# Attention with a gated MLP on one core: loads of the output weights in head order, x in halves, and a new matmul order in the last stage

## The chip, the cores and the metric

The kernel runs on one core of a Trainium2 chip. The metric is device time in microseconds (us) of one execution, the median of many. Most executions of a kernel agree within about 0.3%. PE is TensorE (matmuls), PEld its weight loads, DVE VectorE, ACT ScalarE, POOL GpSimd, and SPq the queue on which the Sync engine issues DMAs.

## The reference

```python
x  = A_x                                   # (1, 2048, 512) bf16
xn = layernorm(x)
q  = xn @ wq                               # 32 heads of 128
k, v = last 512 rows of the caches         # 8 kv heads, each used by 4 heads
o  = softmax(q k^T / sqrt(128)) v          # per head
s  = concat(o) @ wo                        # (4096, 512)
g  = silu(silu(xn @ w1) @ w2)              # MLP 512 -> 1792 -> 512
return x + s * g
```

## The kernel before

The tokens are worked in 4 blocks of 512. A *step* is one head of one block, 128 steps in all. In each step PE computes a query projection (L207), four score matmuls (L229), four probability-times-value matmuls of the head three steps back (the *PV product*, L271), and filler: the MLP in block 0, the output projection of the block before (L328) later. ScalarE takes the exponentials, VectorE normalises them, and one transposing DMA per step, the *flip* `pT<-p_all`, turns them for the PV product. A flip is issued on SPq, in order with every other load on that queue:

```python
def flip(s):
    pT[s] = work.tile([P, NKC, BLK], BF16, name="pT", tag="pT", bufs=3)
    nc.sync.dma_start_transpose(
        pT[s].rearrange("p kc (j q) -> p (kc j) q", q=P), p_all[s][:, :, :, :]
    )
```

The output weights wo (32 heads of 128 KB) come on the same queue, over tiles that the MLP has left. Seven heads share one tile, in an order that forces some 384 KB to be loaded as two DMAs of 256 and 128 KB:

```python
WO_HOME = {"big0": (0, 1, 2, 3, 4, 5, 12), "big1": (6, 7, 8, 9, 10, 11, 13), ...}   # cut

wo_plan = {                       # at the end of step: [(first head, heads), ...]
    HQ - 5: [(0, 4)],
    HQ - 4: [(4, 2), (12, 1)],
    HQ - 3: [(6, 4)],
    HQ - 2: [(10, 2), (13, 1)],
    HQ + 1: [(14, 4)],
    HQ + 3: [(18, 2), (26, 1)],
    HQ + 5: [(20, 4)],
    HQ + 7: [(24, 2), (27, 1)],
    HQ + 9: [(28, 2), (30, 2)],
}
```

The output projection of the last block is not done head by head. It is a 2 x 2 scheme with seven products, m1 to m7, in place of eight. Each is two PSUM groups of 16 matmuls with 256 columns, one per pair of heads. VectorE prepares operands (`row_sums`, `diag`, `skew`) from the head outputs and combines the results. It begins while the last three PV products are still waiting for their flips:

```python
for u in pv_units(NSTEP - 2): u()              # the PV product before the last
for p in range(6, 12): diag(p)                 # VectorE
m34[4, 1] = bank("sc", [P, HALF], "m4_ps")
for p in range(EARLY): mm(m34[4, 1], 4, p, 1)  # 14 matmuls
for t in range(2):
    for p in (HP - 2, HP - 1): mm(m34[3, t], 3, p, t)   # 4 matmuls
for u in pv_units(NSTEP - 1): u()              # the last PV product
... # m5, rest of m4, then skew(0..9), m2, m1, m7, m6; cut
```

The softmax here doesn't subtract the row's maximum and nothing guards it: scores larger than these inputs give would overflow.

## Time and profile before

| | before |
|---|---|
| median of the executions first given, then of those timed beside the change | 555.18, 554.98 us |
| span of the profile | 552.5 us |
| PE busy | 541.3 us, 98% |
| PE waiting for flips, sum in the list of waits | 2.0 us in 3 waits |
| granted clock | 1.0 |

From the page of before: the span, the busy time per engine, and the chain that ended last, as shares of the span.

```profile
span 552.5 us, 8484 instructions
PE 541.3 (98%) x2629; PEld 260.7 (47%) x2676; DVE 461.0 (83%) x1261; ACT 387.5 (70%) x1122; POOL 20.4 (4%) x41
PE 91%; DMA 5%; DVE 1%; ACT 1%; issue 1%
```

PE is nearly always busy, so what can be gained without removing matmuls is the little time in which it isn't. From the timeline of PE in before, two windows. The columns are start, length, engine, line, operation, and in brackets the idle time just before and what ended it.

```profile
230.96 0.38 PE L229 MATMUL sc_ps<-kT,qT 128*128 128x512 bf16 x1
232.26 0.60 PE L271 MATMUL o_ps<-pT,v 128*128 128x512 bf16 x2 [0.92 <-DMA pT<-p_all]
...
528.90 0.27 PE L464 MATMUL m_ps<-wq_sum,oT 128*128 128x256 bf16 x1
529.82 1.02 PE L271 MATMUL o_ps<-pT,v 128*128 128x512 bf16 x4 [0.65 <-DMA pT<-p_all]
```

The bracket understates such a wait, because a matmul's shown length (0.38 us) runs past the start of the next one: matmuls of 512 columns start every 0.216 us, those of 256 every 0.109. This document therefore counts a wait as the distance of two starts less that pitch: 232.26 - 230.96 - 0.216 = 1.08 us, and 529.82 - 528.90 - 0.109 = 0.81 us. (The tables take starts to the nanosecond, hence 1.09.)

From the timeline of VectorE in before: its last instructions.

```profile
547.14 0.69 DVE L492 SCALAR_TENSOR_TENSOR x_t<-c,x_t 128x512 bf16<-128x512 f32 x1
547.75 0.42 DVE L488 TENSOR_TENSOR m<-m_ps,gate 128x256 f32<-128x256 f32 x1
548.20 0.42 DVE L585 SCALAR_TENSOR_TENSOR x_t<-m,c 128x256 bf16<-128x256 f32 x1
548.78 0.42 DVE L488 TENSOR_TENSOR m<-m_ps,gate 128x256 f32<-128x256 f32 x1 [0.16 <-PE m_ps L464]
549.24 0.43 DVE L585 SCALAR_TENSOR_TENSOR x_t<-m,c 128x256 bf16<-128x256 f32 x1
```

It waits only 0.16 us for PE: it is nearly a second limit of the last stage.

### The profile page before, as it was taken

Reading aid. Unit: us, or ns where it says so; the run is one execution under the profiler, and the core shown is the slowest. Engines: PE = TensorE matmul, PEld = TensorE weight load, DVE = VectorE, ACT = ScalarE, POOL = GpSimd, SP = SyncE. Lnnn points to the kernel's source line nnn. Section 1 sums busy time; section 2 is a strip of 40 time slices with the busy share of each in tenths; the row PEclk is TensorE's granted clock in tenths of the full one; section 3 lists DMA queues with packets and bytes.
Section 4 is the critical chain, followed back from the end, with each engine's and each line's share of the span. In section 5 each row is a group of like instructions: output and inputs, shape, how many; then the busy total and the mean of one; then the engine's idle time right before and its main releaser. Section 6 shows DMA issues by size and latency. Waiting matters only on the chain.

```text
span 552.5 us, 8484 instructions
## 1 busy us (share of the span) xinstructions
PE 541.3 (98%) x2629; PEld 260.7 (47%) x2676; DVE 461.0 (83%) x1261; ACT 387.5 (70%) x1122; POOL 20.4 (4%) x41
## 2 busy tenths in 40 slices
PE   8999999999999999999999999999999999999997
PEld 5644444444444444444444444444444444444576
DVE  6888978967896788798889888988889889888887
ACT  5458657756776677777777777777788888788600
POOL 1000000000000000010001000100010001000000
PEclk9999999999999999999999999999999999999999
DMA  9748697886859799979798979897989887988931
GB/s 295 184 104 171 132 194 150 175 171 135 161 114 182 181 208 222 205 147 185 153 149 162 183 154 150 162 184 153 152 160 178 160 146 158 179 154 134 182 87 39
DMA packets 297901, 89.69 MB, mean 162 GB/s; under 512 B 282368, under 2 KB 296960, under 8 KB 297856
## 3 DMA queue, kind: packets, MB, share of 16 engines
q1 hardware_dynamic: 296128, 85.09, 80.5%
q0 software_dynamic: 1312, 3.67, 2.5%
q8 instruction: 21, 0.34, 0.3%
q10 hardware_dynamic: 416, 0.39, 0.2%
q14 instruction: 24, 0.20, 0.1%
HBM read 17.30 MB, written 2.10 MB: 35 GB/s over the span
## 4 chain that ended last, share of the span: by engine, by line
PE 91%; DMA 5%; DVE 1%; ACT 1%; issue 1%
PE sc_ps L229 19%; PE o_ps L271 19%; PE q_ps L207 19%; PE s_ps L328 14%; PE oB_ps L176 9%; PE h_ps L144 6%; DMA pT<-p_all 5%; PE m_ps L464 4%; PE h_ps L658 2%; ACT th L154 1%; DMA x<-in_A_x_dram 1%; ACT p_all L232 0%; DVE hT L155 0%; DVE st L108 0%; PE t_ps L622 0%
## 5 line engine op out<-in xcount | busy, mean ns | idle before, releaser
L232 ACT ACTIVATE p_all<-sc_ps 128x512 bf16<-128x512 f32 x512 | 304.9, 597 | 99.0 <-PE sc_ps L229 84.4
L229 PE MATMUL sc_ps<-kT,qT 128*128 128x512 bf16 x512 | 193.7, 379 | 0.7
L244 DVE TENSOR_SCALAR p_all<-p_all,rden 128x512 bf16<-128x512 bf16 x512 | 157.8, 351 | 9.1
L271 PE MATMUL o_ps<-pT,v 128*128 128x512 bf16 x498 | 134.3, 379 | 2.6 <-DMA pT<-p_all 2.0
L207 PE MATMUL q_ps<-xnT,wq 128*128 128x512 bf16 x501 | 135.0, 379 | 0.5
L277 DVE CAST oT<-o_ps 128x512 bf16<-128x512 f32 x128 | 88.2, 689 | 44.0 <-PE o_ps L271 41.5
L232 ACT ACTIVATION_READ_ACCUMULATOR p_all<-sc_ps 128x1 f32 x512 | 101.0, 197 | 0.0
L328 PE MATMUL s_ps<-wo_big,oT 128*128 128x512 bf16 x326 | 97.8, 379 | 0.5
L271 PEld LDWEIGHTS <-v 128*128 128x128 bf16 x512 | 49.5, 98 | 63.6 <-DMA pT<-p_all 5.1
L229 PEld LDWEIGHTS <-qT 128*128 128x128 bf16 x512 | 50.1, 98 | 61.6 <-issue 1.8
L219 DVE CAST qT<-q_ps 128x512 bf16<-128x512 f32 x112 | 77.0, 687 | 2.5 <-PE q_ps L207 2.5
L207 PEld LDWEIGHTS <-wq 128*128 128x128 bf16 x512 | 50.1, 98 | 61.0 <-issue 1.0
L176 PE MATMUL oB_ps<-w,hT 128*128 128x512 bf16 x215 | 62.6, 379 | 0.3
L328 PEld LDWEIGHTS <-oT 128*128 128x128 bf16 x384 | 37.6, 98 | 45.3
L144 PE MATMUL h_ps<-xnT,w 128*128 128x512 bf16 x165 | 51.5, 379 | 0.6 <-DVE hT L155 0.3
L242 DVE RECIPROCAL rden<-den 128x2 f32<-128x2 f32 x256 | 40.5, 158 | 10.3 <-ACT p_all L232 10.3
L155 DVE SCALAR_TENSOR_TENSOR hT<-th,h_ps 128x512 bf16<-128x512 bf16 x42 | 28.8, 685 | 7.2 <-ACT th L154 6.9
L176 PEld LDWEIGHTS <-hT 128*128 128x128 bf16 x224 | 21.9, 98 | 26.2
L154 ACT ACTIVATE th<-h_ps 128x512 bf16<-128x512 f32 x42 | 25.1, 599 | 6.6 <-PE h_ps L144 5.7
L144 PEld LDWEIGHTS <-w 128*128 128x128 bf16 x168 | 16.4, 98 | 20.0 <-issue 0.4
L185 ACT ACTIVATE th<-oB_ps 128x512 bf16<-128x512 f32 x16 | 9.5, 595 | 18.0 <-PE oB_ps L176 17.2
L345 POOL DMA_DIRECT2D out_dram<-x_e x12 | 6.6, 549 | 316.2 <-DVE rden L242 303.4
(63 smaller groups left out, 236.0 us busy)
## 6 DMA issues: line engine op xcount, KB each, us to landing
wq<-in_A_wq_dram SPq DMA_DIRECT2D x8, 512.0 KB, 3.9
w<-in_B_w_dram SPq DMA_DIRECT2D x3, 896.0 KB, 10.3
pT<-p_all SPq DMA_TRANSPOSE x128, 4.4
wo_big<-in_A_wo_dram SPq DMA_DIRECT2D x4, 512.0 KB, 4.2
x<-in_A_x_dram SPq DMA_DIRECT2D x3, 512.0 KB, 10.2
x_e<-in_A_x_dram POOLq DMA_DIRECT2D x12, 128.0 KB, 3.1
out_dram<-x_e POOLq DMA_DIRECT2D x12, 128.0 KB, 2.2
v<-in_A_v_cache_dram SPq DMA_DIRECT2D x8, 128.0 KB, 3.9
```

Of the source, the lines that this page charges most:

```text
L144: nc.tensor.matmul(h_ps[:, lo : lo + n], w1_sb[f // FH][:, c, (f % FH) * P : (f % FH + 1) * P], xnT[b][:, c, lo : lo + n], start=(c == 0), ...
L154: nc.scalar.activation(th, h_ps, ACT.Tanh, scale=0.5)
L176: nc.tensor.matmul(cur["ps"], hT[b][f // 2][:, f % 2, j * P : (j + 1) * P], w2_sb[f // FH][:, f % FH, :], start=(f == 0), stop=(f == NFC - 1),
L207: nc.tensor.matmul(cur["ps"], wq_sb[h // REP][:, c, (h % REP) * DH : (h % REP + 1) * DH], xnT[b][:, c, :], start=(c == 0), stop=(c == ND - 1),
L219: nc.vector.tensor_copy(qT[s], cur["ps"])
L229: nc.tensor.matmul(sc, qT[s][:, j * P : (j + 1) * P], kT[h // REP], start=True, stop=True)
L232: nc.scalar.activation(p_all[s][:, :, j, :], sc.rearrange("p (kc q) -> p kc q", q=P), ACT.Exp, scale=INV_SQRT_DH, accum_out=den[s][:, j : ...
L242: nc.vector.reciprocal(rden, den[s][:, j0 : j1 + 1])
L244: nc.vector.tensor_scalar_mul(p_all[s][:, :, j, :], p_all[s][:, :, j, :], rden[:, j - j0 : j - j0 + 1])
L271: nc.tensor.matmul(cur["ps"], v_sb[h // REP][:, kc, :], pT[s][:, kc, :], start=(kc == 0), stop=(kc == NKC - 1))
L277: nc.vector.tensor_copy(oT[s // 2][:, s % 2, :], cur["ps"])
L328: nc.tensor.matmul(acc[j], oT[(b * HQ + h) // 2][:, h % 2, j * P : (j + 1) * P], wo_of(h), start=(h == 0), stop=(h == HQ - 1),)
```

## The change

Its intent is to take PE's last waits away: put more matmuls between the last two PV products, and let the loads of wo disturb the flips less.

```diff
     def load_x(b):
         new_x(b)
-        nc.sync.dma_start(x_blk[b], x2[...].rearrange("(j p) d -> p j d", p=P))
+        xv = x2[ds(b * BLK, BLK), :].rearrange("(j p) d -> p j d", p=P)
+        for j in range(0, BLKT, BLKT if b == 1 else 2):
+            n = BLKT if b == 1 else 2
+            nc.sync.dma_start(x_blk[b][:, j : j + n, :], xv[:, j : j + n, :])
 ... WO_HOME
-        "big0": (0, 1, 2, 3, 4, 5, 12),       # and so on
+        "big0": tuple(range(0, 7)),           # 7..13, 14..20, 21..27
 ... B_PAIRS regrouped to suit (cut)
 ... wo_plan
-            HQ - 4: [(4, 2), (12, 1)],
-            HQ - 3: [(6, 4)],
-            HQ - 2: [(10, 2), (13, 1)],
+            HQ - 4: [(4, 3)],
+            HQ - 3: [(7, 4)],
+            HQ - 2: [(11, 3)],
             HQ + 1: [(14, 4)],
-            HQ + 3: [(18, 2), (26, 1)],
-            HQ + 5: [(20, 4)],
-            HQ + 7: [(24, 2), (27, 1)],
-            HQ + 9: [(28, 2), (30, 2)],
+            HQ + 3: [(18, 3)],
+            HQ + 5: [(21, 4)],
+            HQ + 7: [(25, 3)],
+            HQ + 9: [(28, 2)],
+            HQ + 10: [(30, 2)],
 ... tail, around the last PV product (cut)
+        for t in range(2):
+            group(5, t, "f")                  # m5: one PSUM bank per half
+        run(5, 0, EARLY[:14])
+        run(5, 1, EARLY[:4])                  # 18 matmuls of m5 before it
+        for p in range(4):
+            skew(p)                           # VectorE, before the last cast
         for u in pv_units(NSTEP - 1):
             u()
+        run(5, 1, EARLY[4:])                  # 10 matmuls ready at once
+        ...                                   # last pairs of m3, m4, m5 and 14 of m2 interleaved
-        tt(c12, m5, a, ALU.add)
-        tt(d, m5, b, ALU.add)
+        for t in range(2):
+            tt(c12[:, t, :], acc[5, t], a[:, t, :], ALU.add)
+            tt(d[:, t, :], acc[5, t], b[:, t, :], ALU.add)
```

In effect there are four edits: x blocks 2 and 3 in halves; wo in head order with four pairs of loads merged; the last two loads of wo on two steps (the *split*); and the tail.

## The prediction

> **What bounds the kernel now.** TensorE. The page gives PE 541.3 us busy of a 552.5 us span (98%) at full granted clock, and the chain that ended last is 91% PE. In the timeline 128x512 matmuls start every 0.216 us and the 256-column ones of the tail every 0.109 us, nearly without a gap. Outside the start (7.2 us) and the end (3.8 us after the last matmul) PE waits for little: the list of waits has 2.0 us of PE on the transposing DMA of the probabilities (pT<-p_all) in three places. The timeline puts them at 232.26 us (0.92 us), 482.25 (0.45) and 529.82 (0.65). So the ceiling is about 2 us, 0.4%.
>
> **What the change does.** No matmul is added or removed: the order listing has 5354 rows on PE before and after, 981 against 983 on VectorE, 82 against 79 on the SP queue.
>
> 1. Tail. Between the last two PV products stand 18 small matmuls; now 32. 14 x 0.109 = 1.5 us more cover, against 0.65 us of waiting: the wait at 529.82 should go, and the last matmul end about 0.8 us earlier (0.65 shown, the rest start-up of the waiting weight load). But VectorE is nearly the limit there: from 536.1 to 549.7 us it has a single gap, 0.16 us. Two 128x512 additions (0.60 us apart) become four of 128x256 (some 0.38 apart): +0.3 us. Skew and diagonal work (0.34 and 0.2 us each) moves ahead of the last cast, into 1.74 us of idle time. I estimate that VectorE's closing chain starts 0.8 us earlier and ends 0.3 to 0.6 us earlier.
>
> 2. Loads of wo. Bytes are the same; four 3-tile loads replace four pairs of loads, which saves issue time on a queue off the critical path. The last 512 KB, two 256 KB loads issued back to back at 223.6 and 224.7 us, are split over two head steps. The flip issued right behind them (225.28 us) took 6.94 us to land against a median of 4.4, and is the one PE waits for at 232.26. The Trainium skill (DMA: Bandwidth & Descriptors, "Issuing engines are not separate DMA queues") says that all transfers run on the same 16 DMA engines and interleave; this trace agrees: flips behind 384-512 KB loads land in 5.0 to 6.5 us. With half the bytes ahead, an estimated 4.8 to 5.5 us: the 0.92 us wait should shrink to at most 0.2. A 16 KB instruction fetch (229.65 us) fell into the same flip, so part may stay.
>
> 3. Loads of x blocks 2 and 3 in halves: landed at 18.0 and 20.7 us, first read at 27.1. Nothing.
>
> 4. Another grouping of pairs for the weight differences: same VectorE work, nothing.
>
> The wait at 482.25 stays (a flip of 7.41 us, with an instruction fetch at 480.4 in it and no wo load).
>
> **Sum.** 0.8 us (wait at 232) + 0.5 us (tail) = 1.3 us of 555.18: predicted 553.9 us, 8 in 10 between 552.9 and 555.2. Faster by over 2%: 0.01; within 2%: 0.98; slower by over 2%: 0.01.
>
> **Right or wrong in the profile.** PE waits for pT fall from 2.0 to some 0.5 us with the one at 482 left; no gap before the last PV; last matmul about 1.7 us earlier, last VectorE instruction 1.0 to 1.5 us earlier; VectorE gaps below 0.5 us in the last 12 us.
>
> **What would make it wrong.** The instruction fetch still delays the flip at 225 us; waits reappear at other flips, since the slack between a flip's landing and its PV product is set by PE's own pace; the longer VectorE queue delays the last cast; VectorE ends the tail no earlier.

## The result, and the profile after

| | before | after |
|---|---|---|
| median | 554.98 us (15 runs) | 551.74 us (10 runs) |
| ratio, 95% interval | | 0.9946 (0.9937 to 0.9955) |
| span of the profile | 552.5 us | 549.3 us |
| PE busy | 541.3 us | 540.8 us |
| granted clock | 1.0 | 1.0 |

Ratios are the mean time of one kernel's runs over that of the other's in the same rounds, so not quite the ratio of the medians. Executions over 1.5% slower than the fastest of the same kernel are left out of the means. The gain is 0.54%, about 3.0 us, where 1.3 were predicted; 551.74 lies below the stated range.

From the page of after: the same lines as of before.

```profile
span 549.3 us, 8482 instructions
PE 540.8 (98%) x2628; PEld 261.0 (48%) x2676; DVE 461.1 (84%) x1263; ACT 388.2 (71%) x1122; POOL 20.3 (4%) x41
PE 91%; DVE 4%; DMA 3%; issue 1%; ACT 1%
```

The same work, and a chain whose DMA share fell from 5% to 3% while VectorE's rose from 1% to 4%: VectorE now holds the end. From the timeline of PE in after, the windows that answer to the two waits (PV products at 230.75 and 528.51 us):

```profile
230.54 0.38 PE L230 MATMUL sc_ps<-kT,qT 128*128 128x512 bf16 x1
230.75 1.03 PE L272 MATMUL o_ps<-pT,v 128*128 128x512 bf16 x4
...
526.48 2.13 PE L465 MATMUL m_ps<-wo_big,s 128*128 128x256 bf16 x18
528.51 1.04 PE L272 MATMUL o_ps<-pT,v 128*128 128x512 bf16 x3
529.38 1.25 PE L465 MATMUL m_ps<-wo_big,s 128*128 128x256 bf16 x10
```

The wait at 232 is gone: 230.75 follows 230.54 at the usual pitch. So is that before the last PV product: 18 matmuls from 526.48 take 18 x 0.109 = 1.96 us, so 0.07 is left. From the timeline of VectorE in after, its last instructions:

```profile
545.12 0.42 DVE L489 TENSOR_TENSOR m<-m_ps,gate 128x256 f32<-128x256 f32 x1
545.57 0.42 DVE L594 SCALAR_TENSOR_TENSOR x_t<-m,c 128x256 bf16<-128x256 f32 x1
545.96 0.42 DVE L489 TENSOR_TENSOR m<-m_ps,gate 128x256 f32<-128x256 f32 x1
546.42 0.43 DVE L594 SCALAR_TENSOR_TENSOR x_t<-m,c 128x256 bf16<-128x256 f32 x1
```

VectorE has no gap left, and ends at 546.85, 2.82 us earlier than before. The span ends 2.46 us after that, where it was 2.83. So one part of the gain, 0.37 us, lies *behind* the last instruction that computes anything; the prediction had nothing there.

### The profile page after: what moved, and what is told of

Same layout as the page of the kernel before. It is cut to its first block, busy times and chain, and to the rows that moved or that the text cites. A ratio compares the mean times of both kernels' runs of the same rounds, so it can differ in the third digit from the quotient of the medians.

```text
span 549.3 us, 8482 instructions
## 1 busy us (share of the span) xinstructions
PE 540.8 (98%) x2628; PEld 261.0 (48%) x2676; DVE 461.1 (84%) x1263; ACT 388.2 (71%) x1122; POOL 20.3 (4%) x41
## 4 chain that ended last, share of the span: by engine, by line
PE 91%; DVE 4%; DMA 3%; issue 1%; ACT 1%
PE o_ps L272 20%; PE sc_ps L230 20%; PE q_ps L208 19%; PE s_ps L329 14%; PE oB_ps L177 9%; PE h_ps L145 6%; PE h_ps L667 2%; DMA pT<-p_all 2%; PE m_ps L465 2%; DVE c L489 1%; DVE s L442 1%; ACT th L155 1%; ACT p_all L233 0%; DVE hT L156 0%; DMA x<-in_A_x_dram 0%
```

## The experiments

Two theories stood. A: the change is worth what its removed waits are worth, and the rest of what the two profiles differ by is chance of single profiles. B: the whole difference is made by the change. Each run below gave one profile, and all but one were timed in five rounds. All gave correct results. The table collects, for all of them, the three quantities that turned out to matter. A wait is start to start less the pitch; below 0.06 us it counts as 0. "End gap" is from the end of VectorE's last instruction to the end of the span, both taken from the trace to the nanosecond. Each profile is of one execution, and the executions of one kernel differ by 1 to 3 us, so a single row is weak; what repeats over rows counts.

| kernel | what it is | ratio (95% interval) | wait near 232 us | wait before last PV | end gap |
|---|---|---|---|---|---|
| before | | | 1.09 | 0.81 | 2.83 |
| ctrl_before | before, again | 1.0015 (1.0002 to 1.0027) | 1.36 | 1.40 | 2.82 |
| tail_only | tail alone | 0.9989 (0.9976 to 1.0001) | 1.04 | 0 | 2.84 |
| loads_only | all but the tail | 0.9978 (0.9966 to 0.9990) | 0 | 0.91 | 2.47 |
| split_only | split alone | 0.9986 (0.9970 to 1.0001) | 0.90, at 236 | 1.31 | 2.83 |
| split_again | the same | one run | 0.90, at 236 | 1.61 | 2.84 |
| wo_only | wo edits alone | 0.9976 (0.9959 to 0.9992) | 0 | 1.26 | 2.59 |
| after | the change | 0.9946 (0.9937 to 0.9955) | 0 | 0.07 | 2.46 |
| after_again | the same | 0.9950 (0.9936 to 0.9964) | 0 | 0 | 2.46 |
| after_nosplit | change, split undone | 0.9957 (0.9941 to 0.9973) | 0 | 0 | 2.48 |
| unmerged | and merging undone | 0.9968 (0.9953 to 0.9982) | 1.10 | 0 | 2.73 |
| before_x6 | before, x in 8 pieces | 0.9990 (0.9976 to 1.0004) | 0.79, at 204 | 1.34 | 2.47 |
| tail_cover | part of the tail alone | 0.9997 (0.9979 to 1.0015) | 1.86 | 0 | 2.84 |
| after_spread | change, more loads spread | 0.9948 (0.9932 to 0.9963) | 0 | 0 | 2.46 |

### The control, and the change again

Edit: none (ctrl_before, after_again).

> The kernel before, submitted unchanged, as a control. Both theories: ratio 1.000 within 0.001. Theory A (the extra gain that the prediction missed is chance of single profiles: first x tile landing at 3.5 or 3.1 us, the waits at 73 and 482 us): a second profile of the same kernel shows the start, the 73 us wait and the 482 us wait differently, by 0.2 to 0.5 us each. Theory B (the extra gain is made by the change): the second profile repeats the first one's waits: about 0.2 us at 73, 0.9 at 232, 0.3 at 253, 0.45 at 482, 0.65 before the last PV product.

> The changed kernel, unchanged, for a second profile. If the waits of single profiles are chance in part: time again 0.994 to 0.996 of before, but the wait at 73 us is back (0.2 to 0.7 us in the four other profiles, none in the first one of this kernel). What should repeat: no wait at 232 us, 0.3 us or less before the last PV product, and 2.46 us from VectorE's last instruction to the end of the span (2.82 before).

The control against itself gave 1.0015, and its interval just misses 1. So a ratio here is good to about 0.0015, or 0.8 us, and only the profiles can settle the parts. Theory A was half right. Some waits are chance: one of 0.62 us at 482 us in the first profile of before is absent from the second (only one other kernel, wo_only, shows it), and the one at 73 us is 0.2 and 0.48 us in the two of before, 0 and 0.57 in the two of after. The start varies too: VectorE's first instruction on x came at 3.55 and 3.34 us in before, 3.14 and 3.20 in after, since the first x tile landed that much earlier or later. But the wait at 232, the last-PV wait and the end gap repeat. In the control both waits are larger than the first profile had them; the last-PV wait is 0.81 to 1.61 us in the seven profiles that keep the old tail, mean 1.23. The first profile was the smallest of the seven.

### The halves of the change

Edits: tail_only is before with only the tail hunks; loads_only is the change with the tail hunks left out.

> Only the new order of the last stage, loads as before. Theory A: 0.75 us off (ratio 0.9986), the wait before the last PV product gone, the wait at 232 us as before. Theory B: the tail gives more than its 0.75 us, up to 1.5 us, because VectorE's last instruction and the closing store also end earlier.

> Everything but the tail: x in halves, wo in head order, the last pair of loads in two steps. Theory A: 1.0 to 1.1 us off (ratio 0.998), the wait at 232 us gone and nothing else that lasts. Theory B: about 2.3 us off (ratio 0.996), with the waits at 73 and 482 us gone too.

The times, 0.9989 and 0.9978, add up to 0.33%, less than the 0.54 of the change but not clearly less in view of the control. In the profiles each half removes its own wait and no other, and the end gap belongs to the loads, not to the tail. Theory B fell in its particulars: the wait at 73 us is 0.74 us in loads_only, and the tail gives no more than its wait. The last matmul stands 1.2 us before VectorE's end in both, as in before. The profiles also give the worth of the tail without adding up waits: from the PV product at 456-458 us to VectorE's end it is 91.1 to 91.6 us in the six kernels with the full tail and 92.2 to 93.6 us in the seven profiles with the old one. The means, 91.4 and 92.7, lie 1.3 us apart, or 1.2 once the waits between 465 and 520 us, which vary from profile to profile, are taken off. The time of tail_only by itself (0.6 us less, 0 to 1.3) is too coarse to say more.

### What of the loads: the split, or the merging

```diff
# split_only, split_again: before with
-            HQ + 9: [(28, 2), (30, 2)],
+            HQ + 9: [(28, 2)],
+            HQ + 10: [(30, 2)],
# after_nosplit: the change with these lines the other way round
# wo_only: before with the WO_HOME, B_PAIRS and wo_plan hunks
```

> Before with one line changed: the two 256 KB loads of heads 28-29 and 30-31 on two head steps. Theory A: 0.9 to 1.1 us off (ratio 0.998), all that the loads give. Theory B: less than half of what loads_only gives, the rest coming from x in halves or from the order of wo.

> A second profile of split_only: the wait stays at about 0.9 us, at 232 or 236 us, if the split alone does not remove it; no wait if the first profile was chance.

> The changed kernel with the two loads of heads 28-29 and 30-31 back on one head step; the other loads of wo stay in order. If the split is what removed the wait at 232 us: it is back with about 1 us, and the time is 1 us longer than that of after_again. If the order and the merging of the other loads did it: no wait at 232, same time. The 2.46 us at the end stay in either case, since the number of loads on the SP queue is the same.

> Before with all the wo edits (order, merging, split), x and the tail as before. The end: the SP queue has 4 DMAs fewer than before. The eight completion semaphores of that queue are taken in turn, and the closing waits test them in fixed order, so the last store should be tested 6th of 8 (second in before, 8th in the full change): the end gap falls from 2.82 to about 2.58 us, neither 2.82 nor 2.46. The wait at 232 us: none or below 0.4, as in loads_only; split alone moved it to 236.

The prediction had laid the whole gain at 232 us on the split. The split isn't needed for it, and in the two profiles of the split alone it isn't enough. From the timelines of PE in split_only and in after_nosplit:

```profile
235.07 0.38 PE L229 MATMUL sc_ps<-kT,qT 128*128 128x512 bf16 x1
236.19 0.61 PE L271 MATMUL o_ps<-pT,v 128*128 128x512 bf16 x2 [0.73 <-DMA pT<-p_all]
```

```profile
230.68 0.38 PE L230 MATMUL sc_ps<-kT,qT 128*128 128x512 bf16 x1
230.90 1.03 PE L272 MATMUL o_ps<-pT,v 128*128 128x512 bf16 x4
```

With the split alone, the wait moves one step on, behind the second load, 0.90 us in both profiles. The flip at 226 us, now with half the bytes ahead of it, does about what the prediction estimated: it lands 4.78 and 4.55 us after its issue. But the next one, behind the second load, takes 6.55 and 6.34 us, and it is this one that shares its flight with an instruction fetch (below). Both profiles are of slow executions: in split_only it was the slowest of six (555.68 us, the others 553.18 to 554.74), so that the split alone helps in other executions is not ruled out. With both loads on one step but the others merged, there is no wait. What is left is the head order and the merging:

```diff
# unmerged: after_nosplit with
-            HQ - 4: [(4, 3)],
+            HQ - 4: [(4, 2), (6, 1)],
-            HQ - 2: [(11, 3)],
+            HQ - 2: [(11, 2), (13, 1)],
-            HQ + 3: [(18, 3)],
+            HQ + 3: [(18, 2), (20, 1)],
-            HQ + 7: [(25, 3)],
+            HQ + 7: [(25, 2), (27, 1)],
```

> after_nosplit with its four 3-tile loads of wo issued as 2 + 1 tiles again, still in head order. Theory A (each extra issue keeps the SP queue busy for some 0.6 us and so the flips behind it later): the wait near 232 us is back with 0.7 to 1.4 us. Theory B (the head order of wo, or chance, removed it): no wait there. The end: four more DMAs on the SP queue, so the last store is tested 4th of 8: end gap 2.71 us (2.46 in after_nosplit).

From the timeline of PE in unmerged:

```profile
231.06 0.38 PE L230 MATMUL sc_ps<-kT,qT 128*128 128x512 bf16 x1
232.37 0.39 PE L272 MATMUL o_ps<-pT,v 128*128 128x512 bf16 x1 [0.93 <-DMA pT<-p_all]
```

Same bytes, same order, same addresses, four more DMA issues, and the wait is back with 1.10 us. Seven of the eight profiles with pairs of loads have a wait of 0.9 to 1.9 us at 232 or 236 us, and none of the six with merged loads has one. The eighth, before_x6, waited 0.79 us at 204 us instead; that flip was issued as early against PE as in the merged kernels, so the pairs did not make this wait. So the merging is what removed the wait at 232. The times alone would not show it: unmerged (0.9968) and after_nosplit (0.9957) differ by 0.6 us, with intervals that overlap. (Merging without head order can't be tried: one DMA needs the three heads side by side.)

Why do four issues of a few hundred nanoseconds matter? From 196 to 231 us the queue is full, most of it with the flips' own issues of 1.8 to 3.7 us each. From the timelines of the SP queue in unmerged and in after_nosplit, the first pair of that stretch (the length is the time that the queue's issue took):

```profile
203.67 1.54 SPq L306 DMA_DIRECT2D wo_big<-in_A_wo_dram  x2
205.33 3.11 SPq L251 DMA_TRANSPOSE pT<-p_all  x1
```

```profile
203.23 0.94 SPq L306 DMA_DIRECT2D wo_big<-in_A_wo_dram  x1
204.33 3.07 SPq L251 DMA_TRANSPOSE pT<-p_all  x1
```

Two loads hold the queue for 1.66 us, the merged one for 1.10. Against PE's progress (as in the table below) the flip before them leaves at -2.98 and -3.04 us, nearly together; the flip behind them at -1.77 and -2.39, 0.62 later with the pair. And since the queue has no gap in which to catch up, it is still 0.65 at the flip in question, 20 us on. The same queue at the second pair, in before and in after_nosplit:

```profile
214.83 1.81 SPq L250 DMA_TRANSPOSE pT<-p_all  x1
216.69 1.63 SPq L305 DMA_DIRECT2D wo_big<-in_A_wo_dram  x2
218.49 5.10 SPq L250 DMA_TRANSPOSE pT<-p_all  x2
223.63 1.54 SPq L305 DMA_DIRECT2D wo_pair<-in_A_wo_dram  x2
225.28 9.01 SPq L250 DMA_TRANSPOSE pT<-p_all  x3
```

```profile
214.42 1.89 SPq L251 DMA_TRANSPOSE pT<-p_all  x1
216.36 1.08 SPq L306 DMA_DIRECT2D wo_big<-in_A_wo_dram  x1
217.56 5.26 SPq L251 DMA_TRANSPOSE pT<-p_all  x2
222.87 1.54 SPq L306 DMA_DIRECT2D wo_pair<-in_A_wo_dram  x2
224.57 9.26 SPq L251 DMA_TRANSPOSE pT<-p_all  x3
```

Each entry starts within 0.2 us of the end of the last one, which reads as flips issued when the queue gets to them and not when their data is ready. Two loads take it from 216.69 to 218.49 in before, 1.80 us; the merged one from 216.36 to 217.56, 1.20 us. (In unmerged this second pair took only 1.28 us; its lateness is from the first.) The rest is in the trace's issue and landing times, here told against PE's own progress: all times are from the start of the PV product before the one in question, which is due 3.45 us later.

```
kernel          flip issued   landed   in flight   16 KB instruction fetch
before            -2.44        4.50      6.94      in the flight
ctrl_before       -2.10        4.76      6.87      in the flight
tail_only         -2.40        4.44      6.84      in the flight
tail_cover        -1.99        5.27      7.25      in the flight
unmerged          -2.23        4.50      6.74      in the flight
before_x6         -3.21        2.46      5.67      just after it landed
after_nosplit     -2.88        1.95      4.83      after it landed
after             -3.38        1.43      4.81      after it landed
loads_only        -3.38        1.43      4.81      after it landed
wo_only           -3.38        1.38      4.76      after it landed
```

Two things come together. With pairs of loads the flip leaves later (2.0 to 2.4 us ahead of the PV product before, against 2.9 to 3.4; before_x6, which had waited at 204 us, apart). And, still under way some 230 us into the run, it is met by a fetch of instructions. The Trainium skill (Runtime: NRT & Kernel Launch, "Instruction fetch mechanics") says that each engine's instruction memory is refilled in blocks of 16 KiB, 256 instructions, by a DMA queue of its own. The trace agrees: in before, single packets of 16,384 bytes come every 24 to 30 us between 65 and 509 us, near the 27.6 us that 128 weight loads and 128 matmuls take at 0.216 us a pair. Such a packet took 0.9 to 1.6 us in before, and a transfer counts as landed only when all its engines have finished (Trainium skill, DMA: Bandwidth & Descriptors, "Why a DMA increments its semaphore by 16 and not by 1"). In before, the flip's first engine reported at 230.18 us and its last at 232.22, with the fetch starting at 229.65. It was not one engine that came late behind the packet: two reported by 230.27, and the other 14 between 232.09 and 232.22. Why one packet holds back nearly all of them is not shown. That flights with a fetch are longer is: in all 14 profiles, between 240 and 505 us, the flips that follow two other flips on the queue took 4.31 us in the median where no fetch started during the flight (936 of them), and 5.59 us where one did (136). The run before_x6 shows this flip's flight without the fetch: with the same pair of loads ahead, the fetch came at 231.32, after the flip had landed at 231.22, and the flight was 5.67 us. PE did not wait there. (It had waited at 204 us, where another fetch met another flip for 7.57 us; that is why this flip's issue is early against PE.) From these numbers an estimate: issued at -2.44 as in before but in flight for 5.67, the flip would land at 3.23, just in time; issued at -3.38 but in flight for 6.9, it would land at 3.5, just about in time too. So neither the lateness nor the fetch alone would cost much, and together they cost a microsecond. In the merged kernels the fetch meets the next flip instead, 1.9 to 3.8 us into its flight (4.4 to 5.2 in the five profiles above that have it in this flip); that one takes 5.5 to 6.0 us, and none of the six makes PE wait. How much is due to each part can't be tried, because the fetch can't be moved at will.

### The end gap

```diff
# before_x6: before with
-        nc.sync.dma_start(x_blk[b], ...)                     # one DMA for each x block
+        for j in range(0, BLKT, BLKT if b == 1 else 1):      # blocks 2 and 3 in four
+            n = BLKT if b == 1 else 1
+            nc.sync.dma_start(x_blk[b][:, j : j + n, :], xv[:, j : j + n, :])
```

> Before with x blocks 2 and 3 each loaded in four pieces: six more DMAs on the SP queue and nothing else. If the order in which the closing waits test the eight completion semaphores makes the difference at the end: the last store is tested 8th of 8 and the end gap is 2.46 us, with all other waits of before (73, 232, 529 us) in place. If the end gap came from the stores or from wo: 2.82. Time: 0.4 us off at most, within the noise.

The idea came from the trace's records of the closing waits of the Sync engine. In before (semaphore numbers after the time; the last store's completion is on 102, and it lands at 551.23):

```
549.70  last store issued, completion on semaphore 102
550.21  wait 100 done
551.25  wait 102 done      <- the last store has landed
551.31  wait 103   551.37  wait 104   551.43  wait 106
551.49  wait 108   551.55  wait 109   551.61  wait 110
```

The DMAs of this queue take eight semaphores in turn: 100, 102, 103, 104, 106, 108, 109, 110. The closing waits test them in this fixed order, about 0.061 us each. When the last store holds the second of them, six more tests follow after it has landed. In before_x6 six more DMAs went before, so it holds the eighth:

```
549.95  last store issued, completion on semaphore 110
550.83  wait 109 done (and all before it)
551.51  wait 110 done      <- the last store has landed
```

The end gap is 2.47 us against 2.83, with nothing else done. The count of DMAs explains every kernel: second of eight in before (2.82 to 2.84), fourth in unmerged (2.73; expected 2.71), sixth in wo_only (2.59; expected 2.58), eighth in loads_only, after and before_x6 (2.46 to 2.48). In the change, +2 for x in halves and -4 for the merging step the last store back by two, from second to eighth. Whether that was meant can't be known; it is what x in halves does for the time.

### The tail: is the cover enough?

```diff
# tail_cover: before with
+        m5 = bank("f", [P, 2, HALF], "m5_ps")
+        for p in range(14):
+            mm(m5[:, 0, :], 5, p, 0)
         for u in pv_units(NSTEP - 1):
             u()
 ...
-        m5 = bank("f", [P, 2, HALF], "m5_ps")
-        for p in range(8):
-            mm(m5[:, 0, :], 5, p, 0)
 ...
-        for p in range(8, HP):
+        for p in range(14, HP):
             mm(m5[:, 0, :], 5, p, 0)
```

> Before with only the cover of the tail: 14 matmuls of group 5 moved ahead of the last PV product, all VectorE work in its old order. The wait before the last PV product (0.8 to 1.4 us in five profiles) should go in either case. Theory A (the rest of the tail change, which moves VectorE work ahead of the last cast, is needed): VectorE's ten skews still follow the last cast, which now comes later, so its last instruction ends at most 0.3 us earlier than in before relative to the PV product at 457 us, and stands over 1.5 us behind the last matmul (1.2 in before). Theory B (only the cover matters): the same gain as tail_only, 1.1 us, and VectorE 1.2 us behind the last matmul.

The wait before the last PV product is gone, as with the full tail, and the time is that of before (0.9997). From the timeline of PE in tail_cover, and then that of VectorE:

```profile
531.15 1.03 PE L271 MATMUL o_ps<-pT,v 128*128 128x512 bf16 x4
532.01 0.27 PE L464 MATMUL m_ps<-xnT_sum,oT 128*128 128x256 bf16 x1
532.96 0.28 PE L464 MATMUL m_ps<-wq_sum,oT 128*128 128x256 bf16 x1 [0.68 <-DVE oT L277]
```

```profile
549.09 0.42 DVE L488 TENSOR_TENSOR m<-m_ps,gate 128x256 f32<-128x256 f32 x1
549.54 0.43 DVE L585 SCALAR_TENSOR_TENSOR x_t<-m,c 128x256 bf16<-128x256 f32 x1
549.88 0.42 DVE L488 TENSOR_TENSOR m<-m_ps,gate 128x256 f32<-128x256 f32 x1
550.33 0.42 DVE L585 SCALAR_TENSOR_TENSOR x_t<-m,c 128x256 bf16<-128x256 f32 x1
```

The gain was given back in two places. PE now waits 0.84 us (532.96 - 532.01 - 0.109) right after the last PV product, for VectorE's cast of it: the matmuls that used to fill that hole had been moved ahead. And VectorE, with all ten skews still behind the later cast, has no gap and ends 1.60 us after the start of the last matmul, against 1.2 in before. From the PV product at 457-458 us to VectorE's end it is 92.57 us, and 92.58 and 92.63 in the two profiles of before; with the waits of PE for flips between 470 and 520 us taken off, 92.2 against 91.8 and 92.3. So theory A holds. The full tail needs its other parts: ten matmuls of m5 that need nothing new right after the last PV product, and four skews and two diagonals ahead of the last cast.

### Spreading more loads

```diff
# after_spread: the change with
-            if s % REP == 1 and s < HQ and s // REP + 2 < HKV:
-                load_head_group(s // REP + 2)                 # k, wq and v together
+            if s % REP >= 1 and s < HQ and s // REP + 2 < HKV:
+                load_head_part(s // REP + 2, s % REP - 1)     # k, wq, v on three steps
```

> The changed kernel with the idea of its split carried to the head-group loads (k, wq, v of a group: 128 + 512 + 128 KB, issued together every fourth head step; here one on each of three steps). If flips delayed behind bunched loads are what PE waits for: the wait at 73 us (0 to 0.7 us) is gone in this profile, and the time is 0.3 to 0.5 us below after_again. If the flip there is late for the instruction fetch alone, the wait stays.

There is no wait at 73 us in this profile. But there was none in two others without the edit (after, after_nosplit), and the time is that of after_again (0.9948 against 0.9950). It is harmless and not shown to help. No version that beats the change was found.

## Why the prediction was wrong

**The direction and the two waits were right.** The waits at 232 us and before the last PV product went, no other wait of PE is shown to have changed, and what is left of them is 0 to 0.07 us.

**The tail was sized too small: 0.5 predicted, about 1.2 measured.** Two steps failed. One: "0.65 us of waiting" was read from a single profile, as the idle column shows it. Start to start it was 0.81, which the prediction allowed for with its "about 0.8 us", but over seven profiles with the old tail it is 0.81 to 1.61, mean 1.23; the profile at hand was the lowest. Two: the discount for VectorE ("ends 0.3 to 0.6 us earlier") was not paid. VectorE was rightly named as nearly the limit, and tail_cover shows that it takes the whole gain where its work isn't moved. But the change moves enough of it ahead of the last cast: in after VectorE still ends 1.2 us after the start of the last matmul, as before, so PE's whole saving reached the end.

**The wait at 232: 0.8 predicted, 1.09 and 1.36 measured in before (0.90 to 1.86 over the seven profiles with pairs that wait at 232 or 236 us, mean 1.18), and the wrong edit credited.** "With half the bytes ahead ... the 0.92 us wait should shrink to at most 0.2" failed as a step: that flip did land as estimated (4.55 and 4.78 us), but with the split alone the wait moved to the next flip, at 236 us, and was 0.90. That the wait went all the same is luck for the prediction: the change held the merging too. What removed it was the merging, which the prediction dismissed with "saves issue time on a queue off the critical path". That queue issues the flips, and in this stretch it is the flips' limit: with the pairs back, the flip left 0.65 us later and PE waited 1.10 us. The instruction fetch that the prediction saw in the flip did have a part, and it ceased to matter once flips left earlier.

**The end: 0 predicted, 0.37 measured.** "3. Loads of x blocks 2 and 3 in halves ... Nothing" was right about x and wrong about the kernel: the number of DMAs on the queue, modulo eight, decides at which of the closing waits the last store is tested.

**The ceiling "about 2 us" failed** for these reasons: it took one profile's waits as the waits, and took the time after the last matmul as fixed.

**The sum.** 1.23 (last PV) + 1.18 (near 232) + 0.37 (end) = 2.8 us, with mean waits. Measured: 0.54% of 555 us = 3.0 (2.5 to 3.5), and 2.8 (2.0 to 3.6) for the second timing. That closes within the noise. What the waits at 73 and 482 us and the start add is not shown to differ between the kernels. Why the wait at 73 us is there in 11 of the 14 profiles and absent from three stays open. "The wait at 482.25 stays" was wrong as put: it is chance, seen in 2 of the 14.

## What to carry to other kernels

When a kernel's busiest engine waits only a microsecond here and there, take the size of a wait from several profiles and from start to start; a single one can be off by half. A queue that issues time-critical transfers is on the critical path, even if its engine computes nothing: there, fewer and larger loads can be worth more than spreading the same bytes, and a transfer that leaves half a microsecond earlier can escape a collision that costs two. Filling a wait with work taken from behind it gains only if something else fills the hole it came from, and if the second-busiest engine's work moves too.

## What the Trainium skill lacked or had wrong

- DMA: Bandwidth & Descriptors, "Issuing engines are not separate DMA queues", calls the sequencer's issue time "usually small relative to the DMA itself". That holds for one wo load here (0.6 to 1.2 us of queue time against 3.2 to 4.2 us to landing). The section doesn't say that such times add up for what stands behind on a queue without gaps: here it was full from 196 to 231 us, and with four issues more the flip left 0.65 us later against PE's progress (unmerged: -2.23 us against -2.88 in after_nosplit). PE waited 1.10 us more.
- Runtime: NRT & Kernel Launch, "Instruction fetch mechanics", calls the cost of crossing a 16 KiB boundary "mostly hidden". Its effect on other transfers is missing: with the same loads ahead, a flip took 5.67 us when the fetch came after it and 6.7 to 7.3 us in the five profiles in which the fetch came during its flight; between 240 and 505 us, with no loads just ahead, the medians are 4.31 and 5.59 us.
- No page has the closing waits: eight DMA semaphores tested in fixed order at about 0.061 us each, so that the end moves by 0.37 us (2.83 to 2.46) with the count of DMAs modulo eight.
